# A causal attention kernel followed by a hard-swish MLP: the mask of pairs four to seven moved from products to selects, with the front of two queues reordered

## The chip, the core and the metric

The kernel runs on one core of one Trainium2 chip. Times are device microseconds from start to end of one execution. Six runs of the kernel before took 354.53 to 354.9 us, with a median of 354.7 us.

The engines are named as in the profile: PE is TensorE (PEld its weight load), DVE is VectorE, ACT is ScalarE, POOL is GpSimd, and SP is SyncE, which here only issues DMAs. A `q` behind an engine's name means its instruction queue.

## The reference

```python
def _attn_ref(q, k, v, s):                       # 8 batches, 8 heads, 576 tokens, 64 wide
    scores = np.matmul(q, k.transpose(0, 1, 3, 2)) / np.sqrt(D)
    cum = np.cumsum(np.maximum(s, 0.0), axis=-1)
    bias = -(cum[:, :, :, None] - cum[:, :, None, :])
    scores = np.where(causal, -1000000000.0, scores + np.minimum(bias, 0.0))
    ...
    attn = attn / (np.sum(attn, axis=-1, keepdims=True) + 1e-09)
    return np.matmul(attn, v)

def _moe_ref(x, w_in, w_out):                    # 4608 tokens, 512 -> 2048 -> 512
    h = x @ w_in
    g = h * np.clip(h + 3.0, 0.0, 6.0) / 6.0
    return g @ w_out
```

`causal` marks the keys that come after the query. The attention output, with the heads side by side, is the input `x` of the second part.

## The kernel before

**Tiling.** The 64 heads are handled two at a time, as 32 pairs `p`; four pairs make a batch of 576 tokens. One turn of the loop over `p` is called a slot here. In a slot TensorE computes the scores of both heads of the pair, transposed (keys on partitions), ScalarE takes their exponential into `P`, and TensorE multiplies `P` with the values (`av`). A column of ones beside the values gives the sum that the result is divided by (`norm`, VectorE). A head's scores come in three groups of 512 columns (`scores(p, hh, g)`): group 0 holds the four 128 x 128 blocks on the diagonal, groups 1 and 2 the blocks off it. The last 64 x 64 corner of both heads has a group of its own (`corner`, into `PC`). Two score banks take turns, so a group waits for the exponential of the second group before it.

**The bias.** The cumulative sums ride in the product: rows 64 to 67 of the tile `qk` (four tiles, used in turn) hold the sums' parts. `load_aug` brings them from `rows_of` with two small DMAs a pair.

**The mask.** The blocks on the diagonal need their upper half shut. For pairs 0 to 7 (`p < NPROD`) a product does it: a matmul of `ident2` with `shut` opens the bank at L377 (512 columns, one for each head) and at L441 (128 columns, one for each pair), and adds a large negative number to what must vanish. From pair 8 on, a select does it: `shut_out` (L426) on GpSimd writes zeros into `P` and `PC` after the exponential. So that the exponential does not overflow there, 60 more rows of `qk` ("stair", rows 68 to 127) push the shut entries down in steps. They come from `stair_sb`, by GpSimd's copies (L695) in slots 5 to 7 and by ScalarE's in slots 8 and 9.

**Query order.** For pairs 3 to 6 (`mixed`) the queries lie in another order within each group of 64, so that the copy from PSUM to `qk` has runs of 16 elements (L298) instead of single elements with a stride of 6 (L310). Their bias rows are in the same order (made by the cast at L840), and `perm` puts the results back when `x` is transposed.

**The second part.** `m1` (L547, then L562 on ScalarE and L563 on VectorE) and `m2` (L574, then L590) are cut into groups of four matmuls of 512 columns. `group()` places one of them into a slot, by a plan written out as a string. The first `m1` groups are in slot four, the first `m2` groups in slot seven. `m1` of block 0 needs a new quarter of `w_in` for every four groups; the first `m2` groups need `w_out` in eight parts.

**Queues.** The order on each engine is the order in which the program is written. GpSimd issues the loads of tokens (`load_qk`, three pairs ahead, with a cast on the way), of `w_in` and `w_out` and most of the bias rows, and it casts the values (`cast_v`). Sync issues the values (`load_v`, two pairs ahead, two buffers), a few bias rows, the results, and the transposing DMAs. `qk_ahead` is the token load of the next pairs. `pool_mid` and `pool_end` hold GpSimd's work in the middle and at the end of a slot; until pair 8 they contain no select.

```python
        if p >= PPB:
            for fn, c in {
                4: ((I, 2),),
                5: ((I, 3),),
                6: ((U, 0), (U, 1), (U, 2), (U, 3)),
                7: ((U, 4), (U, 5), (U, 6), (U, 7)),
            }.get(p, ()):
                fn(c)
        if PPB <= p < NPROD:
            pool_mid()
```

So in slots 4 to 7 the weight DMAs stand before the cast of the next pair's values.

Of the kernel before, what the change touches and what calls it, by code (L numbers as in the profile page):

```python
# [10 lines left out]
F16 = mybir.dt.float16  # L11
# [7 lines left out]
def kernel(  # L19
# [30 lines left out]
    NVRAW = 2  # L50
    VW = 66
    NROW = 1
    NWARM = (11, 2, 6)
    HALVES = (slice(0, 288), slice(288, SEQ))

    grp = (np.arange(128) * 61 // 128)[None, :]
    steps_r = np.arange(1, 61)[:, None]  # L60
    stair = np.zeros((128, 2, 128), np.float32)
    stair[68:, 0] = np.where(grp < steps_r, 1.0, 0.0)
    stair[68:, 1] = np.where(grp == steps_r, NEG_BIG, 0.0)
    stair_dram = nc.inline_tensor(stair.astype(np.float16), name="stair")

    cpool = ctx.enter_context(tc.tile_pool(name="consts", bufs=1))
    work = ctx.enter_context(tc.tile_pool(name="work", bufs=2))
# [24 lines left out]
    shut, shutm = keep("shut", [128, 128], F16, 2)  # L92
    perm = keep("perm", [128, 128], F16)
    ident2 = keep("ident2", [128, 128], F16)
    stair_sb = keep("stair_sb", [128, 2, 128], F16)
    bias3 = keep("bias3", [128, 1], F32)
    rows_of = keep("rows_of", [128, 3, 640], F16, 2)
    sel = keep("sel", [128, 4], F32)
# [60 lines left out]
    def load_aug(p, eng):  # L159
        for hh in range(2):  # L160
            g = 2 * p + hh
            eng.dma_start(  # L162
                out=qks[p % NQK][64:68, hh, :, 64 * hh : 64 * hh + SEQ],
                in_=rows_of[g // 32].rearrange("(r g) i t -> g r i t", g=32)[
                    g % 32, :, slice(0, 3, 2) if mixed(p, 0) else slice(1, 3), 0:SEQ
                ],
            )

    def load_w_in(c):
        nc.gpsimd.dma_start(  # L170
# [100 lines left out]
        return pt  # L271

    def mixed(p, i):
        return i == 0 and PPB - 1 <= p < NPROD - 1

    def mix(ap):
        return ap.rearrange("p (g w v) -> p g w v", w=4, v=16)
# [91 lines left out]
    def scores(p, hh, g):  # L369
        qT, kT = qk_of(p, hh)  # L370
        pt = Pof(p, hh)
        S = s_bank([128, 512], "S")
        by_product = p < NPROD
        if g == 0:
            rows = slice(0, 68 if by_product else 128)
            if by_product:
                mm(  # L377
                    S.rearrange("p (t c) -> p t c", c=128),
                    lhsT=ident2,
                    rhs=(shutm if mixed(p, 0) else shut)[:, None, :].to_broadcast(  # L380
                        [128, 4, 128]
                    ),
                    start=True,
                    stop=False,
                )
            for j in range(4):
                c = slice(128 * j, 128 * (j + 1))
                mm(  # L388
                    S[:, c],
                    lhsT=kT[rows, c],  # L390
                    rhs=qT[rows, c],
                    start=(j == 0 and not by_product),
                    stop=(j == 3 and p >= NROW),
                )
            if p < NROW:
                for j in range(4):
                    c = slice(128 * j, 128 * (j + 1))
                    by_rows(p, hh, S[:, c], c, c, j == 3)
        else:
            for j in ((0, 3) if g == 1 else (1, 2)):  # L400
                c = OFF[j] - 512 * g
                w = 448 - 128 * j
                mm(  # L403
                    S[:, c : c + w],
                    lhsT=kT[0:68, 128 * j : 128 * (j + 1)],
                    rhs=qT[0:68, 128 * (j + 1) : SEQ],
                    start=(c == 0),
                    stop=(c != 0 and p >= NROW),
                )
            if p < NROW:  # L410
                for j in ((0, 3) if g == 1 else (1, 2)):
                    c = OFF[j] - 512 * g
                    w = 448 - 128 * j
                    mm(
                        S[:, c : c + w],
                        lhsT=rows_of[0][:, 2, 128 * j : 128 * (j + 1)],
                        rhs=picked[:, 2 * p + hh, 128 * (j + 1) : SEQ],
                        start=False,
                        stop=(c != 0),
                    )  # L420
        c = slice(512 * g, 512 * (g + 1))
        nc.scalar.activation(out=pt[:, c], in_=S, func=AF.Exp, scale=0.125)  # L422

    def shut_out(ap, w):
        part = ap.rearrange("p (t c) -> p t c", c=w)
        nc.gpsimd.affine_select(  # L426
            out=part,
            in_=part,
            pattern=[[0, part.shape[1]], [1, w]],
            compare_op=ALU.is_ge,  # L430
            fill=0.0,
            base=0,
            channel_multiplier=-1,
        )

    def corner(p):
        S = s_bank([128, 2, 64], "Sc")
        by_product = p < NPROD
        rows = slice(0, 68 if by_product else 128)
        if by_product:  # L440
            mm(  # L441
                S,
                lhsT=ident2,
                rhs=(shutm if mixed(p, 0) else shut)[:, None, 0:64].to_broadcast(
                    [128, 2, 64]
                ),
                start=True,
                stop=False,
            )
        for hh in range(2):  # L450
            qT, kT = qk_of(p, hh)
            if p < NROW:
                by_rows(p, hh, S[:, hh, :], slice(512, 640), slice(512, 576))
            mm(  # L454
                S[:, hh, :],
                lhsT=kT[rows, 512:640],
                rhs=qT[rows, 512:576],
                start=(hh == 0 and not by_product),
                stop=(hh == 1),
            )  # L460
        pc = PCs[p % 2][:, 0:128]
        nc.scalar.activation(  # L462
            out=pc, in_=S.rearrange("p h c -> p (h c)"), func=AF.Exp, scale=0.125
        )
# [225 lines left out]
    make_shut(shutm, mix(shutm), [[64, 2], [1, 4], [4, 16]])  # L690
    nc.gpsimd.tensor_copy(out=unmix(perm), in_=mix(ident))

    def set_stair(i, copy, heads=(0, 1)):
        for hh in heads:
            copy(  # L695
                out=qks[i][64:128, hh, :, 64 * hh : 64 * hh + 640].rearrange(
                    "p i (t c) -> p i t c", c=128
                ),
                in_=stair_sb[64:128, :, None, :].to_broadcast([64, 2, 5, 128]),
            )  # L700

    fill(nc.vector, xT[:, 0, 0:SEQ], 0.0)

    def warm(n):
# [122 lines left out]
    head_out(0, 0, 1, pts[0], (A, V.tensor_copy))  # L827
    head_out(0, 1, 1, pts[1], (V.tensor_copy, V.tensor_copy))
    warm(NWARM[2])
    load_aug(1, nc.gpsimd)  # L830
    load_v(1, nc.sync)
    load_aug(2, nc.sync)
    cast_v(0)
    for i in range(2):
        load_qk(3, i)
    load_v(2, nc.sync)
    cast_v(1)
    for i in range(2):
        load_qk(4, i)
    nc.gpsimd.tensor_copy(  # L840
        out=mix(rows_of[0][0:32, 0, 0:SEQ]), in_=unmix(C["c"][0:32])
    )


    I, U = load_w_in, load_w_out
# [1 line left out]
    for p in range(NP):  # L847
# [25 lines left out]
                crossbar_qk(p + 2)  # L873

        def pool_mid():
            if p >= NPROD:
                shut_out(Pof(p, 0)[:, 0:512], 128)
            if nxt:
                cast_v(p + 1)
            if p in (5, 6, 7):  # L880
                set_stair((p + 3) % NQK, nc.gpsimd.tensor_copy)
            if p == 13:
                new_rest()
                cum4(1, nc.gpsimd, whole)
                cum5(1, nc.gpsimd.tensor_copy, whole)

        def pool_end():
            if p >= NPROD:
                shut_out(PCs[p % 2][:, 0:128], 64)
                shut_out(Pof(p, 1)[:, 0:512], 128)  # L890
            if p >= NPROD and p != 9 and p + 2 < NP:
                if p == 14:
                    cum6(1, nc.gpsimd, whole)
                load_aug(p + 2, nc.gpsimd)

        if p >= PPB:
            for fn, c in {
                4: ((I, 2),),
                5: ((I, 3),),
                6: ((U, 0), (U, 1), (U, 2), (U, 3)),  # L900
                7: ((U, 4), (U, 5), (U, 6), (U, 7)),
            }.get(p, ()):
                fn(c)
        if PPB <= p < NPROD:
            pool_mid()
            if p == 4:
                load_aug(7, nc.gpsimd)
            elif p in (6, 7):
                load_aug(p + 2, nc.gpsimd)

        if p and p + 2 < NP:
# [2 lines left out]
            load_aug(3, nc.sync)  # L914
            load_aug(4, nc.sync)
        if p == 2:
            nc.sync.dma_start(out=stair_sb, in_=stair_dram.ap())
        if p == 10:
            load_s(1, (nc.sync,) * 4)
            fill(nc.gpsimd, rows_of[1][:, 1, :], 1.0)  # L920
# [31 lines left out]
        if p == PPB:  # L952
            early[0] = False
            scores(p, 0, 0)
            av(p - 1, 1, 0)
            av(p - 1, 1, 1)
            norm(p - 1, 1)
            m1_begin(0, 0, NKC - 1)
            scores(p, 0, 1)
            transpose_x(p - 1)  # L960
            m1_begin(0, 1, NKC - 1)
            pt = transpose_in(p + 1, 0)
            transpose_out(p + 1, 0, pt, pars=(0,))
            group()
            transpose_out(p + 1, 0, pt, pars=(1,))
            scores(p, 0, 2)
            group()
        else:
            scores(p, 0, 0)
            if p >= NPROD:  # L970
                pool_mid()
            get(0)
            group()
            scores(p, 0, 1)
            av(p - 1, 1, 0)
            if p >= NPE - 1:
# [6 lines left out]
        if p == 12:  # L983
            cum2(whole)
        corner(p)
        if p in (8, 9):
            set_stair(3, nc.scalar.copy, (p - 8,))
        elif p == 11:
            new_sum()
            cum1(1, whole)  # L990
        group()
# [3 lines left out]
            get(1)  # L995
            av(p, 0, 0)
        scores(p, 1, 0)
        if p >= NPROD:
            pool_end()
        if PPB < p < NPE - 1:  # L1000
            get(1)
        elif p == 3 * PPB:
# [62 lines left out]
```

## Time and profile before

| | us |
|---|---|
| median of six runs | 354.7 |
| the profiled execution: its own time | 354.62 |
| its span, first to last instruction | 352.9 |
| TensorE busy | 344.7 (98%) |
| VectorE busy | 230.3 (65%) |
| ScalarE busy | 224.6 (64%) |
| GpSimd busy | 169.6 (48%) |
| granted TensorE clock | 1.00 |

What lies between the span and the execution's own time, 1.7 us, is outside the instructions. A line of the timeline gives the start, the duration, the engine, the line of the kernel, the operation, what it writes and reads, and in brackets the idle time in front of it with what ended it. A line of the groups gives the busy time, the mean duration of one in ns, and the idle time in front of the group. The matmul durations overlap, so that only the distance from one start to the next is TensorE's price for one.

### The profile page before, as it was taken

What the parts mean: (1) busy time and instruction counts of PE and PEld (TensorE: products, weight loads), DVE (VectorE), ACT (ScalarE), POOL (GpSimd) and SP (SyncE); (2) the same over time, 40 slices, a digit from 0 to 9 for tenths busy, and PEclk for the clock granted to TensorE, in tenths of its full rate; (3) what the DMA queues carried; (4) which work ended last, traced back from release to release, by engine and by line L of the source; (5) the groups of instructions that cost most, each with busy time, mean ns of one, the idle gap of its engine ahead of it and who ended that gap; (6) DMA issues with size and microseconds to landing.
All of it is one profiled execution on the core that took longest, in us unless ns stands there. A gap on an engine that the chain in (4) does not pass through costs nothing.

```text
span 352.9 us, 7778 instructions
## 1 busy us (share of the span) xinstructions
PE 344.7 (98%) x2926; PEld 191.3 (54%) x2926; DVE 230.3 (65%) x476; ACT 224.6 (64%) x397; POOL 169.6 (48%) x296
## 2 busy tenths in 40 slices
PE   7999999999999999999999999999999999999995
PEld 2775666655555555555555555555555444444442
DVE  7996996676868677666666666757654544544531
ACT  6987896787787667666776666666664334444310
POOL 8987699876778556455555555555310000000000
PEclk9999999999999999999999999999999999999999
DMA  8999999999999999999798879695120100101112
GB/s 162 153 208 191 193 172 202 135 181 187 142 151 103 187 221 206 182 189 186 168 164 203 177 168 196 157 201 143 38 75 15 59 26 36 59 2 59 59 47 74
DMA packets 144783, 48.35 MB, mean 137 GB/s; under 512 B 130649, under 2 KB 139785, under 8 KB 144745
## 3 DMA queue, kind: packets, MB, share of 16 engines
q1 hardware_dynamic: 117112, 37.54, 53.7%
q0 software_dynamic: 27392, 10.03, 26.1%
q8 instruction: 23, 0.38, 0.5%
q10 hardware_dynamic: 240, 0.28, 0.2%
q14 instruction: 16, 0.12, 0.1%
HBM read 37.36 MB, written 9.44 MB: 133 GB/s over the span
## 4 chain that ended last, share of the span: by engine, by line
PE 91%; DVE 4%; ACT 2%; DMA 1%; issue 1%; POOL 0%; ACTq 0%; POOLq 0%
PE po L574 35%; PE ph L547 34%; PE O L481 7%; PE S L403 7%; PE S L388 4%; DMA tok<-in_k_dram 1%; DVE qk L310 1%; PE pt L266 1%; ACT P L422 1%; DVE x L504 1%; PE S L377 1%; PE ptx L518 1%; PE Sc L454 1%; ACT tr L562 1%; DVE qk L230 1%
## 5 line engine op out<-in xcount | busy, mean ns | idle before, releaser
L563 DVE SCALAR_TENSOR_TENSOR gT<-tr,ph 128x512 f16<-128x512 f32 x144 | 98.9, 687 | 97.3 <-ACT tr L562 96.2
L547 PE MATMUL ph<-xT,w_in_sb 128*128 128x512 f16 x576 | 148.1, 379 | 0.0
L574 PE MATMUL po<-w_out_sb,gT 128*128 128x512 f16 x576 | 145.8, 379 | 0.0
L562 ACT ACTIVATE tr<-ph,bias 128x512 f32<-128x512 f32 x144 | 99.0, 688 | 73.0 <-PE ph L547 71.1
L422 ACT ACTIVATE P<-S 128x512 f16<-128x512 f32 x192 | 111.3, 596 | 37.6 <-PE S L388 22.4
L547 PEld LDWEIGHTS <-w_in_sb 128*128 128x128 f16 x576 | 51.6, 97 | 44.1
L574 PEld LDWEIGHTS <-gT 128*128 128x128 f16 x576 | 50.2, 97 | 46.4 <-issue 0.2
L426 POOL TENSOR_SCALAR_AFFINE_SELECT P<-P 128x512 f16<-128x512 f16 x48 | 31.1, 648 | 43.8 <-ACT P L422 43.8
L403 PE MATMUL S<-qk 68*128 68x448 f16 (+3 forms) x256 | 48.9, 272 | 0.5 <-ACT P L422 0.5
L481 PE MATMUL O<-va,P 128*128 128x65 f16 x896 | 47.9, 193 | 0.3 <-ACT P L422 0.3
L481 PEld LDWEIGHTS <-P 128*128 128x128 f16 x896 | 39.3, 97 | 14.0 <-ACT P L422 0.5
L230 DVE COPY qk<-jt 64x768 f16<-64x768 f16 x84 | 36.9, 440 | 1.4 <-DMA jt<-tok 0.2
L403 PEld LDWEIGHTS <-qk 68*128 68x128 f16 x256 | 23.7, 98 | 24.4 <-issue 0.9
L162 POOL DMA_DIRECT2D qk<-rows_of x56 | 32.8, 588 | 1.7 <-PE S L403 1.1
L504 DVE TENSOR_TENSOR x<-O,rl 128x320 f16<-128x320 f32 x64 | 31.5, 492 | 2.2
L590 DVE TENSOR_SCALAR ob<-po 128x512 f32<-128x512 f32 (+1 forms) x36 | 24.4, 676 | 8.3 <-PE po L574 7.6
L388 PEld LDWEIGHTS <-qk 128*128 128x128 f16 (+1 forms) x256 | 19.0, 98 | 13.3 <-DVE qk L310 1.6
L426 POOL TENSOR_SCALAR_AFFINE_SELECT PC<-PC 128x128 f16<-128x128 f16 x24 | 7.0, 293 | 39.0 <-ACT PC L462 38.9
L388 PE MATMUL S<-qk 128*128 128x128 f16 (+1 forms) x256 | 24.8, 219 | 0.5 <-DVE qk L310 0.4
L206 POOL CAST va<-vraw 128x512 f16<-128x512 f32 x32 | 20.9, 653 | 7.2 <-DMA vraw<-in_v_dram 7.1
L310 DVE COPY qk<-pt 64x576 f16<-64x576 f16 x22 | 17.6, 805 | 6.2 <-ACT qk L310 5.8
L202 POOL CAST tok<-raw 128x576 f16<-128x576 f32 x28 | 18.0, 679 | 0.0
(79 smaller groups left out, 201.8 us busy)
## 6 DMA issues: line engine op xcount, KB each, us to landing
out_dram<-ob SPq DMA_DIRECT2D x35, 256.0 KB, 2.0
vraw<-in_v_dram SPq DMA_DIRECT2D x64, 128.0 KB, 4.1
raw<-in_q_dram SPq DMA_DIRECT2D x14, 288.0 KB
raw<-in_k_dram SPq DMA_DIRECT2D x14, 288.0 KB
tok<-in_q_dram POOLq DMA_DIRECT2D x18, 144.0 KB, 5.2
tok<-in_k_dram POOLq DMA_DIRECT2D x18, 144.0 KB, 6.1
w_in_sb<-in_moe_w_in_dram POOLq DMA_DIRECT2D x4, 512.0 KB, 8.6
w_out_sb<-in_moe_w_out_dram POOLq DMA_DIRECT2D x8, 256.0 KB, 6.8
```

The lines of the kernel that those rows point to most:

```text
L162: eng.dma_start(out=qks[p % NQK][64:68, hh, :, 64 * hh : 64 * hh + SEQ], in_=rows_of[g // 32].rearrange("(r g) i t -> g r i t", g=32)[g % ...
L230: copies[par](out=qk[0:64, :, i, 128 * par : 128 * par + 256 * n].rearrange("p h (s two c) -> p h s two c", two=2, c=128)[:, :, :, 0, :], ...
L388: mm(S[:, c], lhsT=kT[rows, c], rhs=qT[rows, c], start=(j == 0 and not by_product), stop=(j == 3 and p >= NROW),)
L403: mm(S[:, c : c + w], lhsT=kT[0:68, 128 * j : 128 * (j + 1)], rhs=qT[0:68, 128 * (j + 1) : SEQ], start=(c == 0), stop=(c != 0 and p >= NROW),)
L422: nc.scalar.activation(out=pt[:, c], in_=S, func=AF.Exp, scale=0.125)
L426: nc.gpsimd.affine_select(out=part, in_=part, pattern=[[0, part.shape[1]], [1, w]], compare_op=ALU.is_ge, fill=0.0, base=0, channel_multip ...
L481: mm(o[:, i, :], lhsT=lhsT, rhs=va[:, hh, j, 0:65], **kw)
L504: nc.vector.tensor_tensor(out=X[p][:, :, hh, :], in0=o[:, :, 0:64], in1=rl.to_broadcast([128, 5, 64]), op=ALU.mult,)
L547: mm(ph, lhsT=w_in_sb[:, kc, ft * 128 : (ft + 1) * 128], rhs=xT[:, kc, n * 512 : (n + 1) * 512], start=(kc == 0), stop=(kc == NKC - 1),)
L562: nc.scalar.activation(out=tr, in_=ph, func=AF.Relu, bias=bias3[:, 0:1])
L563: nc.vector.scalar_tensor_tensor(out=gTs[n][:, ft, :], in0=tr, scalar=6.0, in1=ph, op0=ALU.min, op1=ALU.mult)
L574: mm(po, lhsT=gTs[n][:, ft, t4 * 128 : (t4 + 1) * 128], rhs=w_out_sb[:, ft, :], start=(ft == 0), stop=(ft == NFT - 1),)
```

## The change

Four things change. First, pairs 4 to 7 take the select in place of the mask product (`NMASK = 4`), and the stair shrinks to 7 rows, one step for 16 queries. Two constants, one for each query order, are loaded straight into `qk` by Sync (`load_stair`, 7 partitions of 3072 elements); `stair_sb` and its copies on GpSimd and ScalarE go. The select's pattern follows the query order of the pair. Second, pair 2 takes the other query order, too. Third, on GpSimd and Sync: `load_aug(1)` goes from GpSimd to Sync, the cast of the other-order rows moves in front of `cast_v(1)`, `load_aug(2)` behind `load_v(2)`, `load_qk(3)` before `cast_v(0)`, and `load_aug(7)`, `(8)` and `(9)` to Sync. In slots 4 to 7 the weight DMAs stand after the first select and the cast of the next values, and before the selects of the corner and of the second head; `w_out` is spread over slots 5 to 7. Fourth, in slot 4 the third score group comes before the second `m1`, and in slots 6 to 9 the two query copies of the next pair have a group of the second part between them.

```diff
+    NMASK = PPB
+    NSTAIR = 7
...
+    grp = (np.arange(128) // 16)[None, :]
+    steps_r = np.arange(1, NSTAIR + 1)[:, None]
...
+    def load_stair(p, eng):
+        eng.dma_start(
+            out=qks[p % NQK][68 : 68 + NSTAIR], in_=stair_drams[mixed(p, 0)].ap()
+        )
...
     def mixed(p, i):
-        return i == 0 and PPB - 1 <= p < NPROD - 1
+        return i == 0 and PPB - 2 <= p < NPROD - 1
...
-        by_product = p < NPROD
+        by_product = p < NMASK
         if g == 0:
-            rows = slice(0, 68 if by_product else 128)
+            rows = slice(0, 68 if by_product else 68 + NSTAIR)
...
+        if mixed(p, 0):
+            part = part.rearrange("p t (g w v) -> p t g w v", w=4, v=16)
+            pattern = [[0, part.shape[1]], [64, w // 64], [1, 4], [4, 16]]
...
-    load_aug(1, nc.gpsimd)
     load_v(1, nc.sync)
-    load_aug(2, nc.sync)
-    cast_v(0)
+    load_aug(1, nc.sync)
+    load_stair(PPB, nc.sync)
     for i in range(2):
         load_qk(3, i)
+    cast_v(0)
     load_v(2, nc.sync)
+    nc.gpsimd.tensor_copy(
+        out=mix(rows_of[0][0:32, 0, 0:SEQ]), in_=unmix(C["c"][0:32])
+    )
+    load_aug(2, nc.sync)
     cast_v(1)
     for i in range(2):
         load_qk(4, i)
-    nc.gpsimd.tensor_copy(
-        out=mix(rows_of[0][0:32, 0, 0:SEQ]), in_=unmix(C["c"][0:32])
-    )
...
         def pool_mid():
-            if p >= NPROD:
-                shut_out(Pof(p, 0)[:, 0:512], 128)
+            shut_out(p, Pof(p, 0)[:, 0:512], 128)
             if nxt:
                 cast_v(p + 1)
-            if p in (5, 6, 7):
-                set_stair((p + 3) % NQK, nc.gpsimd.tensor_copy)
+            for fn, c in {
+                4: ((I, 2),),
+                5: ((I, 3), (U, 0), (U, 1)),
+                6: ((U, 2), (U, 3), (U, 4)),
+                7: ((U, 5), (U, 6), (U, 7)),
+            }.get(p, ()):
+                fn(c)
...
         def pool_end():
-            if p >= NPROD:
-                shut_out(PCs[p % 2][:, 0:128], 64)
-                shut_out(Pof(p, 1)[:, 0:512], 128)
+            shut_out(p, PCs[p % 2][:, 0:128], 64)
+            shut_out(p, Pof(p, 1)[:, 0:512], 128)
...
         if p == 2:
-            nc.sync.dma_start(out=stair_sb, in_=stair_dram.ap())
+            for i in range(PPB + 1, NPROD):
+                load_stair(i, nc.sync)
+        if p in (4, 6, 7):
+            n = 7 if p == 4 else p + 2
+            if p != 4:
+                load_stair(n, nc.sync)
+            load_aug(n, nc.sync)
+        elif p == 8:
+            load_stair(10, nc.sync)
...
             scores(p, 0, 1)
             transpose_x(p - 1)
+            scores(p, 0, 2)
             m1_begin(0, 1, NKC - 1)
...
-            scores(p, 0, 2)
             group()
         else:
             scores(p, 0, 0)
-            if p >= NPROD:
-                pool_mid()
-            get(0)
-            group()
+            pool_mid()
+            if NPROD - 1 <= p + 1 < NPE:
+                pt = transpose_in(p + 1, 0)
+                transpose_out(p + 1, 0, pt, pars=(0,))
+                group()
+                transpose_out(p + 1, 0, pt, pars=(1,))
+            else:
+                get(0)
+                group()
...
-        if p in (8, 9):
-            set_stair(3, nc.scalar.copy, (p - 8,))
-        elif p == 11:
+        if p == 11:
```

## The prediction

> **What bounds the kernel now.** I read the page first, then TensorE's waits, then its timeline, then GpSimd's. The page's busy shares and its chain that ended last:
>
> ```profile
> PE 344.7 (98%) x2926; PEld 191.3 (54%) x2926; DVE 230.3 (65%) x476; ACT 224.6 (64%) x397; POOL 169.6 (48%) x296
> PE 91%; DVE 4%; ACT 2%; DMA 1%; issue 1%; POOL 0%; ACTq 0%; POOLq 0%
> L377 PE MATMUL S<-shut,ident 128*128 128x512 f16 x16 | 6.1, 379 | 0.0
> L441 PE MATMUL Sc<-shut,ident 128*128 128x128 f16 x8 | 1.8, 219 | 0.0
> L426 POOL TENSOR_SCALAR_AFFINE_SELECT P<-P 128x512 f16<-128x512 f16 x48 | 31.1, 648 | 43.8 <-ACT P L422 43.8
> ```
>
> TensorE is the bound, and GpSimd carries nothing of the chain. So a product taken from TensorE counts in full, unless TensorE then waits for something else. A matmul's own duration is no price, since matmuls overlap; the step from one start to the next is. TensorE's timeline gives the steps and the waits (start, duration, what, wait in front):
>
> ```profile
> 16.27 0.38 PE L403 MATMUL S<-qk 68*128 68x320 f16 x2
> 17.05 0.45 PE L518 MATMUL ptx<-ident,x 128*128 128x128 f16 x5 [0.40 <-DVE x L504]
> ...
> 17.65 0.38 PE L377 MATMUL S<-shut,ident 128*128 128x512 f16 x1
> 18.25 0.40 PE L388 MATMUL S<-qk 68*128 68x128 f16 x4 [0.22 <-DVE qk L310]
> ...
> 20.02 0.38 PE L377 MATMUL S<-shut,ident 128*128 128x512 f16 x1
> 20.24 0.39 PE L388 MATMUL S<-qk 68*128 68x128 f16 x4
> ...
> 30.61 0.20 PE L481 MATMUL O<-va,P 128*128 128x65 f16 x1 [0.34 <-ACT P L422]
> ...
> 32.67 0.38 PE L403 MATMUL S<-qk 68*128 68x320 f16 x2 [0.33 <-ACT P L422]
> ```
>
> From 20.02 to 20.24: a 512-column mask product costs 0.22 us, and a 128-column one 0.06 (29.62 to 29.68). By starts, the waits are 0.56 at 17.05, 0.38 at 18.25, 0.35 at 26.02, 0.50 at 30.61 and 0.49 at 32.67, all before 34 us; after that one is left, 0.38 at 71.32. GpSimd's timeline around slots four to six (slot = pair):
>
> ```profile
> 27.62 0.61 POOL L206 CAST va<-vraw 128x512 f16<-128x512 f32 x1 [1.25 <-DMA vraw<-in_v_dram]
> ...
> 33.69 0.80 POOL L170 DMA_DIRECT2D w_in_sb<-in_moe_w_in_dram  x1
> 38.63 0.61 POOL L206 CAST va<-vraw 128x512 f16<-128x512 f32 x1 [4.13 <-DMA vraw<-in_v_dram]
> 39.34 0.29 POOL L207 CAST va<-vraw 64x128 f16<-64x128 f32 x1
> ...
> 43.34 2.85 POOL L178 DMA_DIRECT2D w_out_sb<-in_moe_w_out_dram  x4
> 46.24 0.61 POOL L206 CAST va<-vraw 128x512 f16<-128x512 f32 x1
> ```
>
> GpSimd stands 4.13 us in front of the cast of pair six's values, until 38.63. Today nothing TensorE needs soon is queued behind that. This is the row on which the forecast turns.
>
> **The change, part by part.**
>
> *Pair two's queries in the other order.* VectorE's two query copies at 14.60 (1.64 us for two, L310) become two of the L298 form (0.91 us at 19.23). VectorE has no gap from there to the key copy that ends at 18.19, and TensorE waits for it at 17.05 and 18.25: 0.73 gained. New is that pair two's bias rows (DMAs of load_aug(2)) wait for the other-order cast of GpSimd. After it cast_v(0) (0.9) and that cast (1.26) follow pair three's token DMAs (2 x 0.67), so it ends near 12.6, Sync issues near 12.7 to 14.1, behind pair two's values (issued at 11.2). The nearest rows are GpSimd's bias rows of 9.4 (landing after 3.3 to 3.7 us) and of 19.7 (6.6 to 6.8, behind tokens). The first gives 17.4 at the latest, when TensorE now comes (17.5); the second 20.7, a loss of up to 3.2 us. I take the first: DMA traffic pauses at 11.5 to 12.2 today, and pair three's tokens, moved forward by 1.2 us, fill that pause instead of competing.
>
> *GpSimd's and Sync's front.* GpSimd loses load_aug(1) (1.18 us), so w_in(0) goes out 1.2 us earlier. Sync takes it near 9.1, where load_aug(2) went before: nothing. Sync also issues one stair DMA there and three after pair four's values (0.6 us each by the stair_sb row at 21.11, which they replace), so pair five's values are issued some 1.2 us later. The cast of pair five runs at 30.45 today without a wait; what is late is absorbed if under about 1 us.
>
> *Masks as selects.* Eight L377 and four L441 go. In slot four the first L377 hides under the VectorE wait at 26.02: nothing. In slots five to seven two each: 6 x 0.216 = 1.29 us. The L441 ones I count at nothing: TensorE has a 0.03 us wait right behind them (37.51 to 37.54) for the exponential that frees the bank. Twelve selects come onto GpSimd: 8 x 0.65 + 4 x 0.29 = 6.4 us, against 7.4 us of L695 stair copies that go. The 4-level pattern of three slots costs a bit more (shutm's select took 0.34 against 0.29).
>
> *Third score group sooner.* The 0.50 wait at 30.61 goes, as exp of group two no longer stands behind tr. But the first m1 moves 0.22 later, and its bank is free only after tr and the L563 product (29.6 + 0.6 + 0.7 = 31.0, where TensorE is at 31.09 today). What is left is read at 32.67: ScalarE loses one exponential between tr and that group, exp at 31.8 to 32.4 instead of 32.6. Gain 0.26.
>
> *Query copies split around a group* (slots six to nine): L563 stands behind two L310 copies at 44.63, and TensorE's 45.38 waits some 0.06 for it; the same at 52.51. 0.12 gained. *ScalarE's L695* (69.39, 1.25 us) is what 71.32 waits for: 0.38 gained.
>
> Sum: 0.73 + 0.26 + 1.29 + 0.12 + 0.38 = 2.78 us, 354.62 - 2.78 = 351.8, if nothing new is waited for. The profiled execution (span 352.9, own time 354.62) lies 0.1 under the median of 354.7.
>
> *The new wait.* A pair's last product block now reads PC after its select, and that select stands behind cast_v(p+1) and the weight DMAs on GpSimd. In slot five: cast 1.0, w_in(3) 0.8, two w_out DMAs 1.4, select 0.3, so PC is ready 3.5 us after pair six's values have landed. TensorE's PC block of slot five starts at 41.12 today and would start at 41.12 - 0.73 - 0.26 - 0.43 = 39.7. So there is no wait if the values land by 36.2; today they land at 38.6. Queued behind TensorE's wait is everything.
>
> Where does that landing go? Today it takes 9.8 us from the issue at 28.25, with tokens and w_in in GpSimd's queue all that time. Here a rule of the Trainium skill speaks the other way. "DMA: Bandwidth & Descriptors", section "Queues, rings and completion order", has each DMA engine take turns between the queues at packet granularity. From 34 to 36 us the trace has 346 packets of q0 (GpSimd's) and 137 of q1 (Sync's). With equal turns, 173 a us, the 1152 rows of 256 B of a pair's values would need 6.7 us and land at 35: no wait, 351.8. The trace's 9.8 decides, since that burst of w_in meets these values again: w_in(2) is now behind a select and a cast, but its data waited for pair seven's tokens anyhow. What shifts is the front: up to 1.2 us earlier from GpSimd, less what the stairs and Sync's later values give back. Bounds: 36.8 and 38.6; I take 37.8, nearest to today's row. PC is ready at 41.3, TensorE waits 1.6 and stands 0.2 behind today there.
>
> After that slots six and seven give 0.86 + 0.12, and 71.32 gives 0.38. In slot six the same queue has cast 1.0, three w_out DMAs 2.15 and select 0.3 behind pair seven's values, which land at 44.3 today (12.7 us from 31.6): ready at 47.7 or sooner, needed at 47.9. Just no second wait. Slot seven has 2 us to spare: values issued near 38 for a cast near 49. Net: 0.2 - 1.36 = -1.2, so 354.62 - 1.2 = 353.4; I say 353.5.
>
> **Rivals.**
> *A: no wait on GpSimd in slots five and six* (values land by 36.2): 351.8. For it: w_in(3) is out of the way, the front is 1.2 us earlier. Against it: w_in(3) never competed with these values (issued at 33.69, behind w_in(2)). 0.18.
> *B: the forecast*, part of the gain given back in slot five: 353.5, own range 352.4 to 354.1. 0.48.
> *C: it is all given back*: values land at 38.6 to 39.2, or the bias rows of pair two come 1 us late and the same wait adds little: 354.2 to 355.2, centre 354.6. 0.20.
> *D, slower:* pair seven's values. w_in(3), w_out(0) and w_out(1) now run back to back from about 39 to 46, where today the queue runs dry near 42.5. If these values land at 47 instead of 44.3, PC of slot six is ready at 50.5, 2.2 us after today's 48.25; 0.87 is won back after it: 354.62 + 2.25 - 0.87 = 356.0. It decides from a landing of 46.4 on. Against it: counted by microsecond, nearly all of Sync's packets for them have started by 42 today. 0.14.
>
> **How the numbers follow.** A, B, C, D: 0.18, 0.48, 0.20, 0.14. About 0.2% (0.7 us) is what a measurement of this kernel can tell from no change. Below 354.0 lie A and nearly all of B, 0.63; within, C and a little of B, 0.23; above 355.4, D, 0.14. The range leaves out the lower half of A and D: 352.0 to 355.0.
>
> **What would show it.** Right: no TensorE wait at ptx near 16.5; S(4) group two exp before tr; a TensorE wait of 1 to 2 us for the select of PC at the end of slot five, with GpSimd's cast of pair six waiting for its values just before; no wait at slot nine. Wrong: a wait of pair two's first product for its rows' DMA; values of pair six landing before 36 (then 351.8); a second long wait in slot six (then slower).

## The result, and the profile after

The changed kernel takes 357.85 us, the median of 18 executions between 354.96 and 360.94; the kernel before took 354.71 in the same job (354.53 to 355.67). The ratio is 1.008, with a 95% interval of 1.0068 to 1.0092: slower, where faster was forecast. (An execution more than 1.5% above the fastest of the same kernel is left out of the ratios.) Two things moved: the median by 3.1 us, and the width of the executions from 1 us to 6. The mean granted clock of the executions goes with their time: it is 1.00 in the two fastest (354.96 and 355.58) and 0.990 to 0.995 in all the others.

The profiled execution took 357.39 us (span 355.6). Its page, busy times and chain; then its list of groups, for the masks:

```profile
PE 344.9 (97%) x2914; PEld 191.8 (54%) x2914; DVE 230.2 (65%) x476; ACT 222.2 (62%) x395; POOL 165.4 (47%) x294
PEclk9998999999999999999999999999999999999999
PE 86%; DVE 3%; DMA 3%; POOL 3%; ACT 3%; issue 1%; SPq 0%; POOLq 0%; ACTq 0%
```

```profile
L389 PE MATMUL S<-shut,ident 128*128 128x512 f16 x8 | 3.2, 400 | 0.0
L459 PE MATMUL Sc<-shut,ident 128*128 128x128 f16 x4 | 0.9, 219 | 0.0
L444 POOL TENSOR_SCALAR_AFFINE_SELECT P<-P 128x512 f16<-128x512 f16 x56 | 37.6, 671 | 49.8 <-ACT P L434 49.8
```

The mask products are halved as planned. But TensorE is busy 344.9 us, not less, although twelve matmuls went; its share of the chain fell from 91% to 86%, while DMA's rose from 1% to 3% and GpSimd's from 0% to 3%. In the clock row one slice has an 8. TensorE's timeline shows where (start, duration, wait in brackets):

```profile
16.63 0.44 PE L536 MATMUL ptx<-ident,x 128*128 128x128 f16 x5
...
17.74 0.40 PE L400 MATMUL S<-qk 68*128 68x128 f16 x4
...
21.14 0.38 PE L389 MATMUL S<-shut,ident 128*128 128x512 f16 x1
24.01 0.38 PE L400 MATMUL S<-qk 68*128 68x128 f16 x4 [2.50 <-DMA qk<-rows_of]
...
26.10 0.63 PE L400 MATMUL S<-qk 68*128 68x128 f16 x4
26.53 0.63 PE L415 MATMUL S<-qk 68*128 68x448 f16 x2
```

The wait at ptx is gone and pair two starts 0.51 sooner (17.74 for 18.25). Then TensorE stands 2.50 us for the bias rows of pair three. And about 2 us after it resumes, the distance from the first diagonal product to the next group, 0.22 before, is 0.43. The windows of one us explain that (busy us of PE, PEld, DVE, ACT, POOL; then the granted clock):

```profile
25.00:26.00 1.00, 1.00 (x27) 0.87 (x25) 0.95 (x3) 1.00 (x4) 1.00 (x2) 0.93 1.37 198
26.00:27.00 1.00, 1.00 (x8) 0.67 (x7) 0.93 (x3) 0.76 (x4) 0.08 (x1) 0.50 1.19 195
27.00:28.00 1.00, 1.00 (x13) 0.88 (x12) 0.90 (x2) 0.95 (x3) 0.61 (x2) 0.50 1.11 171
28.00:29.00 1.00, 1.00 (x17) 1.00 (x16) 0.47 (x2) 0.56 (x1) 0.87 (x2) 0.50 1.24 191
29.00:30.00 1.00, 1.00 (x21) 0.88 (x19) 0.79 (x3) 0.53 (x1) 0.66 (x2) 0.86 1.24 201
```

For 3.4 us TensorE runs at half the clock. That is why its busy time did not fall: it counts slow matmuls as busy. Such a stretch takes 0.005 off the mean clock of an execution of 355.6 us. By that estimate a mean of 0.995 stands for one stretch and 0.990 for two, and all but two of the executions of the changed kernel had at least one.

The distance from the first diagonal product of one pair to that of the next, from the timelines, shows where the time went. The last two columns are two of the experiments told below: the one with the front and slot four in the old order and without the split of the query copies, and the best order found.

| from pair | before | after | old order | best order |
|---|---|---|---|---|
| start to 2 | 18.25 | 17.74 | 18.34 | 18.33 |
| 2 to 3 | 3.80 | 6.27 | 3.82 | 3.82 |
| 3 to 4 | 3.97 | 4.75 | 3.96 | 3.96 |
| 4 to 5 | 8.26 | 8.42 | 8.04 | 8.05 |
| 5 to 6 | 7.08 | 6.65 | 6.65 | 6.65 |
| 6 to 7 | 7.14 | 6.69 | 7.20 | 6.69 |
| 7 to 8 | 8.64 | 9.11 | 8.87 | 9.00 |
| 8 to 9 | 7.19 | 7.15 | 7.15 | 7.15 |
| 9 to 10 | 9.24 | 8.88 | 8.88 | 8.88 |
| 10 to the end | 279.34 | 279.92 | 279.65 | 279.67 |

The two rows of pair three cost 3.25; the gains in slots five, six and nine (1.24) are nearly all lost again in slots four and seven and from slot ten on (1.21).

Who made the rows late? Before, the lines of Sync, GpSimd and TensorE that bear on it were these:

```profile
13.33 0.92 SPq L150 DMA_DIRECT2D vraw<-in_v_dram  x2
16.04 2.54 SPq L162 DMA_DIRECT2D qk<-rows_of  x4
15.93 0.80 POOL L170 DMA_DIRECT2D w_in_sb<-in_moe_w_in_dram  x1
22.05 0.40 PE L388 MATMUL S<-qk 68*128 68x128 f16 x4
```

Sync's and GpSimd's timelines of after:

```profile
14.19 0.93 SPq L157 DMA_DIRECT2D vraw<-in_v_dram  x2
15.21 1.07 SPq L161 DMA_DIRECT2D vraw<-in_v_dram  x1
16.33 3.35 SPq L169 DMA_DIRECT2D qk<-rows_of  x4
```

```profile
14.43 0.79 POOL L182 DMA_DIRECT2D w_in_sb<-in_moe_w_in_dram  x1
...
39.23 0.60 POOL L218 CAST va<-vraw 128x512 f16<-128x512 f32 x1
39.78 0.28 POOL L219 CAST va<-vraw 64x128 f16<-64x128 f32 x1
40.01 0.76 POOL L182 DMA_DIRECT2D w_in_sb<-in_moe_w_in_dram  x1
40.77 1.42 POOL L190 DMA_DIRECT2D w_out_sb<-in_moe_w_out_dram  x2
42.19 0.38 POOL L444 TENSOR_SCALAR_AFFINE_SELECT PC<-PC 128x128 f16<-128x128 f16 x1
```

The rows are issued at 16.33, only 0.3 later than before (16.04), but they are there only 7.7 us after that, at 24.01, where before they had landed by 22.05, within 6.0. In front of them the values of pair three were issued 0.9 later (14.19 for 13.33), and beside them the burst of w_in runs 1.5 earlier (14.43 for 15.93). The rest of the second fence is the place of the forecast's wait in slot five: no wait for values at 39.23, and the select is done before TensorE, late itself, needs it.

### The profile page after: what moved, and what is told of

The parts are those of the page before. It is cut to its first block, busy times and chain, and to the rows that moved or that the text cites. A ratio compares the mean times of both kernels' runs of the same rounds, so it can differ in the third digit from the quotient of the medians.

```text
span 355.6 us, 7772 instructions
## 1 busy us (share of the span) xinstructions
PE 344.9 (97%) x2914; PEld 191.8 (54%) x2914; DVE 230.2 (65%) x476; ACT 222.2 (62%) x395; POOL 165.4 (47%) x294
## 4 chain that ended last, share of the span: by engine, by line
PE 86%; DVE 3%; DMA 3%; POOL 3%; ACT 3%; issue 1%; SPq 0%; POOLq 0%; ACTq 0%
PE po L592 34%; PE ph L565 32%; PE O L499 7%; PE S L415 7%; PE S L400 3%; DMA qk<-rows_of 2%; DVE gT L581 1%; DMA vraw<-in_v_dram 1%; DVE qk L242 1%; ACT tr L580 1%; POOL tok L134 1%; ACT P L434 1%; PE pt L278 1%; PE ptx L536 1%; DVE qk L322 0%
## 5 line engine op out<-in xcount | busy, mean ns | idle before, releaser
L444 POOL TENSOR_SCALAR_AFFINE_SELECT P<-P 128x512 f16<-128x512 f16 x56 | 37.6, 671 | 49.8 <-ACT P L434 49.8
L522 DVE TENSOR_TENSOR x<-O,rl 128x320 f16<-128x320 f32 x64 | 31.5, 492 | 2.2
L169 POOL DMA_DIRECT2D qk<-rows_of x48 | 28.5, 596 | 0.3 <-POOL rows_of L783 0.3
L444 POOL TENSOR_SCALAR_AFFINE_SELECT PC<-PC 128x128 f16<-128x128 f16 x28 | 8.5, 304 | 42.8 <-ACT PC L480 42.7
L400 PE MATMUL S<-qk 75*128 75x128 f16 (+1 forms) x256 | 25.3, 221 | 2.6 <-DMA qk<-rows_of 2.5
L400 PEld LDWEIGHTS <-qk 75*128 75x128 f16 (+1 forms) x256 | 19.1, 98 | 14.6 <-issue 3.0
L322 DVE COPY qk<-pt 64x576 f16<-64x576 f16 x20 | 16.0, 804 | 4.4 <-ACT qk L322 4.1
```

What stands on the lines that cost most here:

```text
L169: eng.dma_start(out=qks[p % NQK][64:68, hh, :, 64 * hh : 64 * hh + SEQ], in_=rows_of[g // 32].rearrange("(r g) i t -> g r i t", g=32)[g % ...
L400: mm(S[:, c], lhsT=kT[rows, c], rhs=qT[rows, c], start=(j == 0 and not by_product), stop=(j == 3 and p >= NROW),)
L444: nc.gpsimd.affine_select(out=part, in_=part, pattern=pattern, compare_op=ALU.is_ge, fill=0.0, base=0, channel_multiplier=-1,)
L522: nc.vector.tensor_tensor(out=X[p][:, :, hh, :], in0=o[:, :, 0:64], in1=rl.to_broadcast([128, 5, 64]), op=ALU.mult,)
```

## The experiments

The ratios are to the kernel before on the same chip, with 95% intervals.

**Rows of pair three ahead of its values** (changed kernel):

```diff
+        if p == 1:
+            load_aug(3, nc.sync)
         if p and p + 2 < NP:
             load_v(p + 2, nc.sync)
         if p == 1:
-            load_aug(3, nc.sync)
             load_aug(4, nc.sync)
```

> Changed kernel, with one move on Sync: pair three's bias rows are issued before pair three's values instead of behind them. Theory 1 (the loss is the wait for these rows, 2.65 us at pair three, and the half clock after it, some 1.75 us): no wait at pair three's first product, granted clock 1.00, time 357.4 - 4.4 = 353.0, range 352 to 354. Rival 2 (the loss is in the selects on GpSimd and the later slots, pair three's wait only hides it): the wait goes, but the selects of slots five and six are waited for instead, 355 or more. Rival 3 (Sync's queue is slow there in any order): the rows land near 24 as well, 357 and more.

Measured: 357.25 us (354.34 to 361.98, 11 executions), ratio 1.0051 (1.0024 to 1.0078). In the profiled execution (355.62) the wait for the rows is gone, pair three starts at 21.45, and a new wait stands behind it:

```profile
25.52 0.31 PE L499 MATMUL O<-va,P 128*128 128x65 f16 x5 [1.48 <-POOL va L218]
```

GpSimd's cast of pair three's values waits for their DMA:

```profile
24.86 0.60 POOL L218 CAST va<-vraw 128x512 f16<-128x512 f32 x1 [4.22 <-DMA vraw<-in_v_dram]
```

In this execution the order on Sync's queue decided which of the two transfers came late. The clock stays at 1.00 behind this shorter wait. The median hardly moved, and 6 of the 11 executions have a mean clock of 0.995 or less: the profiled one is among the better ones.

**The front alone:** the kernel before, with pair two in the other order and the changed front of both queues; products as masks, no stair DMA in the front.

> Kernel before, with only the change's front: pair two in the other query order, and GpSimd's and Sync's front in the new order (no stair DMA, since the masks stay products). Theory 1: pair three waits for its rows by about 2 us, a bit less than in the changed kernel since one stair DMA is missing in front of them, and the clock drops where the wait is long: 355 to 358, slower than before by 0.5 to 3. Rival 2: the front alone gains its 0.7 us, 354.0.

Measured: 357.88 (355.92 to 361.14, 13 executions), ratio 1.0082 (1.0053 to 1.0111): as large as the whole loss. TensorE's timeline, in the profiled execution (359.74):

```profile
25.43 0.38 PE L388 MATMUL S<-qk 68*128 68x128 f16 x4 [3.92 <-DMA qk<-rows_of]
```

Half the clock follows here, too, for 3.4 us from 0.9 us after the resumption. The front consists of several moves (the rows of pairs one and two, the other-order cast, the tokens of pair three ahead of a cast), and no run separates them all.

**All but the front:** the changed kernel with the front of before (the stair of pair four behind `load_aug(2)`) and the other order from pair three on.

> Changed kernel with the front of the kernel before (pair one's rows on GpSimd, pair two's rows ahead of its values, the other order from pair three on); pair four's stair is issued behind pair two's rows. Theory 1: no wait at pair three, clock 1.00, and the masks' gain alone, 1.3 to 2.0 us: 352.7 to 353.5. Rival 2 (selects behind casts and weight DMAs on GpSimd): TensorE waits 1 to 2 us for PC in slot five, 354.5 or more.

Measured: 355.16 (354.05 to 359.35, 20 executions), ratio 1.0032 (1.0006 to 1.0057). The profiled execution (354.63) has no wait at pair three and a clock of 1.00, but still no gain: slot four takes 8.86, slot seven 9.12. Six of the 20 executions still have a mean clock of 0.995 or less. So the front is the larger part of the loss, and the rest is no gain either. The two losses, 0.8% and 0.3%, do not simply add up to the 0.8% of both.

**w_in behind the cast** (changed kernel): `cast_v(2)` before `load_w_in(0)`.

> Changed kernel with the first quarter of w_in issued behind the cast of pair two's values (near 17.3 instead of 14.4); Sync's order is that of the changed kernel. If it is the burst of w_in in GpSimd's queue that holds up Sync's rows (theory 1 as I put it: rows behind values, and values slow beside w_in), the rows land 2 us or more earlier, before 22, the wait at pair three is under 0.5 and the clock stays: 353 to 354.5. If the order on Sync alone sets it (rows behind pair three's values, whatever GpSimd moves), they land near 24 as before: 357.

Measured: 357.97 (355.31 to 359.74, 12 executions), ratio 1.008 (1.0055 to 1.0105). In the profiled execution (355.61) the rows of pair three are in time, with w_in issued at 17.29 and the rows 0.35 later than in the changed kernel (16.68). So w_in's burst has a part in making the rows late. Here pair one's rows were late:

```profile
14.77 0.38 PE L400 MATMUL S<-qk 68*128 68x128 f16 x4 [0.77 <-DMA qk<-rows_of]
```

That wait is not a consequence of this edit: these rows are issued at 9.16 as in the changed kernel, where w_in goes out only at 14.43. It is another transfer of the changed front (pair one's rows on Sync) that came late in this execution. The median did not move, and 7 of the 12 executions have a mean clock of 0.995 or less, so they lose the time in ways that this one profile does not show.

**TensorE fed during the wait** (changed kernel):

```diff
+            for _ in range(11 if (p, hh) == (3, 0) else 0):
+                mm(
+                    S.rearrange("p (t c) -> p t c", c=128),
+                    lhsT=ident2,
+                    rhs=shutm[:, None, :].to_broadcast([128, 4, 128]),
+                    start=True,
+                    stop=True,
+                )
```

> The changed kernel with eleven idle mask products (2.4 us by 0.22 us each) put into pair three's first score bank, where TensorE otherwise stands 2.5 us for the bias rows; their result is overwritten. If the halved clock behind that wait is a cost of its own: no PEclk below 1.0 between 24 and 30 us in the profile, pair four's first product about 1.7 us sooner than in the changed kernel (27.0 instead of 28.76), and a median near 356.2. If the clock has nothing to do with the wait, or the steps behind the wait are slow for another reason (late data): the doubled steps and the time stay, 357.8.

Measured: 356.79 (356.56 to 357.11, 4 executions, all at a clock of 1.00), ratio 1.0051 (1.0034 to 1.0069): the median is 1.06 under that of the changed kernel (measured in another job), with eleven products more. TensorE's timeline, then its windows:

```profile
21.20 2.54 PE L389 MATMUL S<-shut,ident 128*128 128x512 f16 x11
23.57 0.38 PE L397 MATMUL S<-shut,ident 128*128 128x512 f16 x1
23.79 0.39 PE L408 MATMUL S<-qk 68*128 68x128 f16 x4
...
27.75 0.40 PE L408 MATMUL S<-qk 75*128 75x128 f16 x4 [0.42 <-DVE qk L322]
...
43.43 0.20 PE L507 MATMUL O<-va,PC 128*128 128x65 f16 x1 [0.64 <-POOL PC L452]
```

```profile
26.00:27.00 1.00, 1.00 (x22) 0.87 (x20) 0.96 (x3) 1.00 (x4) 1.00 (x3) 1.00 0.76 118
27.00:28.00 1.00, 0.58 (x16) 0.46 (x13) 0.97 (x2) 0.82 (x2) 1.00 (x2) 1.00 1.17 165
```

The clock stays at 1.00, so the half clock came from the idle time. Its price is 1.0 us at pair four (27.75 for 28.76), of which 0.2 is the earlier start of pair three: I had expected 1.7, but at full clock TensorE meets a wait for VectorE's key copy at 27.75 that the slow steps covered. And now that TensorE is sooner, the last line is the forecast's wait, in its place in slot five. GpSimd's timeline of the same run:

```profile
39.39 0.61 POOL L218 CAST va<-vraw 128x512 f16<-128x512 f32 x1 [1.30 <-DMA vraw<-in_v_dram]
40.35 0.29 POOL L219 CAST va<-vraw 64x128 f16<-64x128 f32 x1 [0.34 <-DMA vraw<-in_v_dram]
40.81 0.77 POOL L182 DMA_DIRECT2D w_in_sb<-in_moe_w_in_dram  x1 [0.18 <-issue]
41.57 1.42 POOL L190 DMA_DIRECT2D w_out_sb<-in_moe_w_out_dram  x2
42.99 0.39 POOL L452 TENSOR_SCALAR_AFFINE_SELECT PC<-PC 128x128 f16<-128x128 f16 x1
```

The values of pair six are cast late, two kinds of weight DMAs follow, then the select, then TensorE, 0.80 late by starts.

**Without the split of the query copies** ("all but the front", with `get(0); group()` in slots six to nine as before):

> The masks as selects with the front of before (as in the run with the selects alone), and the two query copies of slots six to nine again without a group between them. Theory: the split keeps the bank of the transposes longer, and the 0.6 to 0.75 us wait of the key transposes in slot seven comes from it; without it that wait goes, pair eight's first product stands near 56.7 instead of 57.3, and the median is 0.5 us under that of the selects alone (355.2), 354.6. Rival: the wait comes from slot six's and seven's other work and stays: 355.2.

Measured: 355.52 (354.63 to 358.81, 20 executions), ratio 1.0025 (1.001 to 1.0041). The expectation failed: slot seven takes 8.87 for 9.12, but slot six 7.29 for 6.69 (7.20 in the next version, which lacks the split, too). The split is a gain of 0.26 to 0.35 in sum. The profiled execution, at 358.1 one of two with a lower clock among the 20, shows the select behind late values once more, a slot earlier than forecast. TensorE, then GpSimd:

```profile
36.27 0.20 PE L499 MATMUL O<-va,PC 128*128 128x65 f16 x1 [1.77 <-POOL PC L444]
```

```profile
34.05 0.61 POOL L218 CAST va<-vraw 128x512 f16<-128x512 f32 x1 [3.27 <-DMA vraw<-in_v_dram]
34.61 0.29 POOL L219 CAST va<-vraw 64x128 f16<-64x128 f32 x1
35.07 0.76 POOL L182 DMA_DIRECT2D w_in_sb<-in_moe_w_in_dram  x1 [0.18 <-issue]
35.85 0.36 POOL L444 TENSOR_SCALAR_AFFINE_SELECT PC<-PC 128x128 f16<-128x128 f16 x1
```

The clock fell to 0.50 there, too, from about 37.1 to 40.5:

```profile
37.00:38.00 1.00, 1.00 (x5) 0.39 (x3) 0.99 (x3) 0.39 (x1) 1.00 (x3) 0.56 0.97 117
38.00:39.00 1.00, 1.00 (x9) 0.50 (x8) 0.06 (x1) 0.47 (x1) 0.99 (x2) 0.50 1.23 197
```

**Slot four in the old order** (the last version, third score group behind the second `m1`):

> As the last, and the third score group of slot four again behind the second m1, as before. Theory: the sooner third group gains nothing, since the two waits of slot four (0.59 and 0.59 by starts) only move and grow; with the old order they are 0.50 and 0.49 again, and pair five's first product stands at 34.5 to 34.7 instead of 34.84: 0.1 to 0.3 us sooner, median 354.3 to 354.5. If the sooner third group was a gain, this is 0.26 us slower than the last run.

Measured: 355.09 (354.26 to 360.28, 12 executions), ratio 1.0005 (0.9992 to 1.0017). Slot four takes 8.04, against 8.86 in "all but the front" (0.53 of that, by starts, is a wait in front of the corner's product, whose select ends just before it) and 8.42 after. The waits of the sooner third group, 0.75 and 0.75 by starts, are 0.55 and 0.71 here. The sooner group is no gain: its two waits are 0.24 longer in sum.

**Casts of values behind the selects** (the last version, slots four to seven):

```diff
         def pool_end():
             shut_out(p, PCs[p % 2][:, 0:128], 64)
             shut_out(p, Pof(p, 1)[:, 0:512], 128)
+            if p < NPROD:
+                cast_v(p + 1)
```

> As the last, and in slots four to seven the cast of the next pair's values goes behind the selects of the corner and of the second head, so that no select stands behind a wait for values. Theory: the wait of the corner's product for its select in slot four (0.36) goes, and with it the dependence on when the values land: no execution above 355.5 and a median of 353.7 to 354.0 (the 0.43 us each of slots five, six and seven that the mask products cost, and a part of slot nine's 0.36, less a stall of some 0.4). If the values themselves are late for their cast, or the spread of the selects alone comes from the front: median as in the last run, executions with a lower clock stay.

Measured: 354.7 (354.14 to 356.84, 12 executions), ratio 0.9991 (0.9965 to 1.0016). No wait of TensorE for a select is left in slots four to seven. But the cast of slot seven comes later (53.34 for 49.77) and frees its buffer later, and Sync issues the values of pair ten at 55.10 instead of 50.40. The transposing DMA of slot nine then lands late, though it is issued only 0.3 later (60.57):

```profile
68.67 0.38 PE L565 MATMUL ph<-xT,w_in_sb 128*128 128x512 f16 x1 [0.60 <-DMA xT<-x]
```

**The best order** (the cast of slot seven in front again; the split in slot six alone):

> The last version (selects with the front and slot four of before, casts of values behind the selects), with two repairs: in slot seven the cast stays in front of the corner's select, so that the values of pair ten are not issued late on Sync (they made the transposing DMA of slot nine late by 0.77 us), and the split of the two query copies is kept in slot six alone. From the traces: with the split slot six took 6.69 and slot seven 9.12, without it 7.20 and 8.87. Expected: 6.7 and 8.9, pair ten's first product near 72.4 instead of 73.57, median 353.7, faster than before by 1.0 us. Rival: the 0.5 us of slot six come back as a longer wait for gT in slot seven, since VectorE is the limit there: 354.2. Second rival: the values land late for their casts in some executions, and the median stays at 354.7.

Measured: 354.71 (353.74 to 359.38, 14 executions; before 354.71), ratio 0.9996 (0.9984 to 1.0008). The profiled execution (353.95) is at 72.53 at pair ten, as expected, without the wait in slot nine. Five executions lie between 353.74 and 353.95; the others lie between 354.59 and 359.38.

**Stairs elsewhere.** Two variants of the best order: the stair of pair four with the others in slot two, and all four in the front behind the rows of pair two.

> As the last, but the stair rows of pair four are loaded with those of pairs five to seven in slot two and no longer in the front of Sync's queue. If that DMA in front of the values of pair two and the rows of pair three is what makes the executions spread, the spread shrinks to that of before (0.4 us for most) and the median falls by up to 0.4 us against the last run; if not, both are equal within 0.2 us.

> As the version with the best order (median 354.71, lowest 353.74), but all four stair rows are loaded by Sync in the front, directly behind the bias rows of pair two, where DMA traffic pauses near 11 to 12 us (busy share 0.38), and none in slot two. Sync issues the values of pair two 0.9 us later (three more issues of 0.3 us). If the spread of the executions comes from the 42 KB stair loads that compete with the values of pairs four and five between 20 and 28 us: most executions at 353.7 to 354.2, median 354.0, faster than before by 0.7 us. If it comes from other loads of that stretch: median 354.7 as without the move. If the values of pair two come late for their cast instead (it waits 0.53 us for them in the kernel before): slower, 355 or more.

Measured: 357.05 (354.38 to 360.09, 22 executions), ratio 1.0043 (1.0028 to 1.0059), and 354.66 (353.84 to 358.22, 14 executions), ratio 1.0006 (0.9988 to 1.0025). In the first, TensorE stands in front of pair four's first product, for which the profile names no releaser; that product's operand is the one that the late stair DMA, issued at 20.73, fills:

```profile
29.38 0.38 PE L400 MATMUL S<-qk 75*128 75x128 f16 x4 [3.66 <-issue]
```

In the second the median and the spread stay: the stair DMAs between 20 and 28 us are not what spreads the executions.

**Pair two in the other order, without the change of Sync's order** (the first of the two, with the cast directly behind `load_aug(1)` on GpSimd):

> As the last, and pair two in the other query order with Sync's order of before: the other-order cast goes directly behind the bias rows of pair one on GpSimd, in front of the first cast of values. Gain if the front holds: pair two 0.5 us sooner (17.7 instead of 18.3) and pair three 0.6 (21.5), at pair ten 0.5 left: median 0.5 us under the last run. Rival: the cast moves every later issue of GpSimd (1.3 us) and Sync's rows of pair two (1 to 2 us), and the rows or values of pairs two and three come late again: slower than the last run by 0.5 to 3 us, with a lower clock in its executions.

Measured: 359.13 (357.81 to 359.42, 5 executions), ratio 1.0116 (1.0101 to 1.013). The rival came true: Sync's first wait is for that cast, and everything behind it slides; the rows of pair three are issued at 18.10.

```profile
25.60 0.58 PE L400 MATMUL S<-qk 68*128 68x128 f16 x4 [4.02 <-DMA qk<-rows_of]
```

Here the clock falls before TensorE resumes, after about 3.1 us of idle time, and is back only at 31.5:

```profile
24.00:25.00 1.00, 0.00 (x0) 0.00 (x0) 0.00 (x0) 0.00 (x0) 0.00 (x0) 0.82 1.37 245
25.00:26.00 1.00, 0.40 (x5) 0.43 (x6) 0.00 (x0) 0.00 (x0) 0.87 (x3) 0.50 1.01 163
```

## Why the prediction was wrong

**The step that failed** is "GpSimd's and Sync's front", priced at nothing; "what is late is absorbed if under about 1 us" was said of pair five's values. The prediction checked the landing of pair two's rows and of those values, and not what stands between them in the same queue: the rows of pair three. The wait there is 2.50 us, and the half clock behind it, for which the sum had no term, 0.8 to 1.0. Moved alone, the front gives a loss as large as the whole; taken back alone, it takes the wait away. It also changes how often the clock falls: a mean of 0.995 or less stands in all but two executions of the changed kernel and in 7 of 13 with the front alone, but in 12 of 92 of the six versions with the old front and the stair of pair four in it. The rows first or w_in later removes the wait for pair three's rows in the profiled execution, but neither repairs the median: in the first the values come late, in the second pair one's rows were. So the front is shown as the larger cause, while which of its transfers is late differs from execution to execution. The prediction saw w_in move 1.2 us earlier and counted it as a relief for later traffic; it was a burst put beside small DMAs with a due time.

**Pair two's other order, 0.73.** Measured 0.51 at pair two, since the key copy, which ends at 17.68, still holds its first product by 0.30; 0.60 at pair three where its rows were in time. Right in kind, and worthless: the cast that it needs stands in front of rows and values in both orders that were tried.

**Masks as selects, 1.29.** By the distances of the table the six products that count lie one in slot four, two each in slots five and six, and one in slot seven. Slot four gains 0.22 (in the old order) and slot five 0.43, as worked out. Slots six and seven together gain next to nothing: they take 15.78 before and 15.69 in the best order. Without the split TensorE waits for gT there (0.39 and 0.30), so that slot six takes 7.20 for 7.14; with it, for the second query copy in slot seven (0.58 in front of the key transposes). The work of VectorE in these slots, which the sum left out, takes that part. L441 at nothing was right; TensorE still stands for some 0.09 at that place.

**Third group sooner, 0.26.** Wrong: one wait moved to the first m1, and both grew (0.75 each by starts).

**Split copies, 0.12.** A gain of 0.51 in slot six and a loss of 0.25 in slot seven; so the 0.45 that slot six gains after is the split's. **Slot nine, 0.38:** 0.36. But 0.2 of it goes in slot ten, to a wait for gT.

**The new wait, 1.6 us for PC's select in slot five.** The mechanism was right and did not decide. It appeared at 0.80 where TensorE came early enough, and at 1.94 by starts in slot four; in the profiled execution after, TensorE was late itself. Moving the casts behind the selects removes it. In the fed run the values of pair six, issued at 28.86, are waited for until 39.39, 10.5 us, where the forecast moved their landing forward to 37.8. The sum for equal turns was too favourable: it gave Sync's queue as many packets as GpSimd's had, 173 a us, and took none from GpSimd's, while the DMA engines were full with 483 packets of both queues in two us. Half of those, 121 a us, would need 9.5 us for 1152 rows (an estimate by count), close to the trace's 9.8. **Rival D** (pair seven's values) did not appear in any profile.

**What stays open.** With the selects in the best order one execution takes 353.74 and another 355.95, both at a clock of 1.00, while the kernel before stays within 1 us in that job (354.48 to 355.44; in the others single executions reach 356 and once 359.41). Which landing differs between executions of that version was not caught in a profile. Five of its 14 executions lie 0.5 to 0.7 us under the fastest of the kernel before; the loss in the others is not explained. Which of the front's moves costs how much stays open, too. No version measured faster than before.

## What to carry to other kernels

When DMA issues are reordered, list every transfer behind the moved one on its queue and every burst that starts sooner, each with its due time and its slack in the trace; here the small rows came late, which the forecast had not listed, and a wait forecast to vanish said nothing of them. Price a long TensorE wait with the slow steps after it: here waits of 1.77 and 2.50 us were followed by them. Look at the width of the executions and at the mean clock of each, not only at one profile: here they showed a loss that single profiles of repaired versions did not.

## What the runs showed of the hardware

- **The clock can fall after a wait of 1.77 us, and after TensorE has resumed.** A wait of 2.50 us gave 3.4 us at 0.50, beginning 1.9 us after TensorE had resumed; one of 1.77 us in slot four, behind two of 0.6, did so as well, 0.9 us after; one of 1.48 us did not. A wait of 3.92 us (the front alone) gave 3.4 us, too, 0.9 us after; in one of 4.02 us (pair two without the change of Sync's order) the clock fell 1.0 us before the resumption and stayed for 6.8 us. The Trainium skill, "TensorE: Matmul & The Clock Gate", Part 1, puts the fall after one idle window of about 3.4 us; here less was enough, and the measurement decides.
- **The select with the pattern of the other query order** takes 0.86 to 0.92 us, against 0.65 for the plain one; the prediction said "a bit more".
- **A 9 KB transfer beside a burst of weights** was there 7.7 us after the first of its pair was issued on Sync's queue; with that burst 2.9 us later it took at most 5.8.
